# Moving the stages of the second half, the solver and the early weights to other slots of a hand-written timetable

## The chip, the cores and the metric

The kernel runs on one core of one Trainium2 chip. The metric is the device time of one execution in microseconds (us), from start to end of the program on that core. The core has five engines with a queue each, worked off in order: PE (matrix products), DVE, ACT and POOL (element-wise work), and SP, which here only issues DMA transfers. They meet through semaphores.

## The reference

Three parts follow each other. First a recurrence over 768 tokens for 4 x 8 heads of dimension 40, then two feed-forward layers over the 3072 tokens of width 320.

```python
for t in range(S):                       # S = 768, per batch and head, state 40x40
    y[t] = r[t] @ state
    Sa   = state @ a[t]
    state = state * w[t] - outer(Sa, b[t]) + outer(v[t], k[t])
x = y.transpose(0, 2, 1, 3).reshape(3072, 320)
h = relu(x @ moe_w_in);  x = (h * h) @ moe_w_out        # 320 -> 2048 -> 320
h = x @ moe2_w_in;       out = (h * cos(h)) @ moe2_w_out
```

## The kernel before

**Chunks.** The recurrence is cut into 12 chunks of 64 tokens (`C = 64`). Within a chunk the sequential part becomes the inverse of a triangular 64x64 matrix per head; only the 40x40 state goes from chunk to chunk. For chunk c+1, `gt` multiplies keys and decayed rows on PE and masks them on DVE into `ga`; `gt_out` writes the triangles to a scratch buffer `Ls` in HBM; `solve_load` reads them back as the tiles `L` and `T` (`lent` for chunk 1, which uses tiles lent by the weights), `corner_load` reads the off-diagonal corner `l21`. `solve` inverts the 32x32 diagonal blocks in 62 small multiply and add steps (L510, L513) and a copy (L517); for chunk 0 on DVE, for all others on POOL. `solve_store` writes the result out, `load_t` reads it back as `t11` and `tt`. `merge(h)` joins the diagonal blocks of one half of the heads: matmuls `pw`, an ACT copy to `l21`, matmuls `pt`, an ACT copy to `tt`.

**Stages.** The 16 head pairs go in four groups g, two to a half. `state(c, g)` is a generator with five stages: `pq` (state times r, not in chunk 0), `px`, `pu` (it uses `tt`, so it needs the merge), `py` with the new state `MT`, and `pm`, which transposes the state. `rv_load`, `mov_load` and `pmat` bring the inputs of a group, `y_store` stores the output of a half to `xs`.

**The timetable.** `period(c)` writes chunk c as 42 slots. `at(t, f)` puts a call into slot t; calls of one slot are emitted in the order in which they were registered. The order in which instructions are emitted is the order in each engine's queue; there is no other scheduler. In each slot, after the calls, `rate[t]` steps of the solver of chunk c+1 are emitted on POOL, then one step of the early weights (`w1`) or of the later ones (`w2`), and from chunk 2 on about 1.5 steps of the feed-forward layers (`mlp`, 64.2 of them to a period). What is left of the layers after chunk 11 runs alone until the end.

**Queues.** Nearly all transfers are issued by SP, one after the other. SP stands still at an instruction whose semaphore is not there yet, and all later transfers stand behind it. `solve_store` is such a place: it needs the end of the solver. The order of SP around it in chunks 2 and later is `y_store`, `solve_store`, `gt_out` (first half of chunk c+2), `load_t`, `gt_out`, then in the next period `load_kb` (`cin`, L379, 832 KB), `rv_load`, in even chunks four loads of `xf` for the layers (`load_x`), `gt_out` (second half), `rv_load`, `mov_load`, `solve_load`.

**Weights.** They arrive as 64-bit numbers. `Weights.first` turns the first 12 of 16 tiles of layer one into 32-bit ones while chunks 0 and 1 run: load, `clamp` on ACT (L171, L172), `bits` on DVE, `add` on POOL (L183), `split` on ACT (L210) and POOL (L215). Its jobs are 5 steps apart. `Vector` (the helper at L146 records all DVE work) inserts the DVE solver of chunk 0 between other DVE instructions.

Of the kernel before, what the change touches and what calls it, by code (L numbers as in the profile page):

```python
# [10 lines left out]
F32 = mybir.dt.float32  # L11
F32R = mybir.dt.float32r
# [146 lines left out]
class Weights:  # L159
# [58 lines left out]
    def first(self, last=NF, layer=0):  # L218

        m, nm = self.m, ("moe", "moe2")[layer]  # L220

        def job(f):
            st = {}

            def load():
                st["dst"] = m.weight_tile(layer, f)
                if self.raw:
                    st["w"] = m.p2.tile([128, 3, 512], F32R, tag=("xh", "xl")[f % 2], name="w1", bufs=1).bitcast(
                        I32).rearrange("p a b -> p (a b)")[:, 0:2 * NW].rearrange("p (a b) -> p a b", b=2)
                    self.load(nm, f, st["w"])  # L230

            def begin(c0, n):
                u = st[c0] = m.p2.tile([128, 512], F32, tag="g", name="u1", bufs=3)[:, 0:n]
                if self.raw:
                    self.clamp(st["w"][:, c0:c0 + n], u)
                else:
                    self.nc.sync.dma_start(u, self.i[nm][f, :, c0:c0 + n])

            out = [(0, load)]
            for t, c0, n in ((5, 0, 384), (6, 384, DM)):  # L240
                out.append((t, lambda c0=c0, n=n: begin(c0, n)))
                if self.raw:
                    out += [(t + 1, lambda c0=c0, n=n: self.bits(st["w"][:, c0:c0 + n], st[c0])),
                            (t + 2, lambda c0=c0, n=n: self.add(st["w"][:, c0:c0 + n], st[c0], st[c0]))]
                out.append((t + 4, lambda c0=c0: self.split(st["dst"], st[c0], c0, layer)))
            return out

        return self.stages([job(f) for f in range(last if self.raw else NF)], 5)

    def pieces(self, nm, tiles, period, end):  # L250

        if not self.raw:
            return iter(())

        def job(f, c0, n):
            st = {}

            def load():
                st["w"] = self.p.tile([128, 256, 2], I32, tag="w", name="w", bufs=2)[:, 0:n]
                self.load(nm, f, st["w"], c0)  # L260

            def clamp():
                st["u"] = self.p.tile([128, 256], F32, tag="u", name="u", bufs=2)[:, 0:n]
                self.clamp(st["w"], st["u"])

# [42 lines left out]
class Attn:  # L308
# [274 lines left out]
    def pmat(self, c, g):  # L583
# [18 lines left out]
        for r0, n, s0 in ((64, 40, 0), (0, 64, 4)):  # L602
            if c:
                nc.scalar.activation(mov[r0:r0 + n, s0:s0 + 4, 64:104], self.MT[g][r0:r0 + n], AF.Copy)
            else:
                nc.gpsimd.memset(mov[r0:r0 + n, s0:s0 + 4], 0.0)

    def y_store(self, c, half):
        for par, r0 in ((0, 64), (1, 0)):
# [3 lines left out]


    def state(self, c, g):
        nc = self.nc
        ga, rv, mov = self.ga[c, g // 2], self.rv.pop((c, g)), self.mov.pop((c, g))
        tt, kc, h4 = self.tt, self.kc, 4 * (g % 2)
# [39 lines left out]
        last = c == self.nch - 1  # L658
        if not last:
            self.vec.tensor_tensor(mt[0:104], yv[0:104, :, 64:104], mt[0:104], op=ALU.add)  # L660
        if c:
            self.vec.tensor_tensor(sz[0:104], yv[0:104, :, 0:64], sz[0:104], op=ALU.add)
        if not last:
            self.vec.tensor_tensor(mt[0:104], mt[0:104],
                                   self.lam[(c + 1) % 3][:, 4 * g:4 * g + 4, 64:65].to_broadcast([104, 4, 40]), op=ALU.mult)
        if g % 2 == 0:
            self.yt = self.p2.tile([128, 8, 64], F32, tag="yt", name="yt", bufs=1)
        yt = self.yt
# [275 lines left out]
def step(gen, n=1):  # L944
    for _ in range(n):
        if next(gen, 0) == 0:
            break

FIRST, RATE = 9, 64.2 / 42


class Program:
# [59 lines left out]
    def run(self):  # L1014
# [56 lines left out]
        self.vec.chain = A.solve(A.nc.vector)  # L1071
        for k in range(10):
            self.vec.credit = 6
            step(g1, 2 if k > 7 else 1)
            if k == 6:
                A.gt_out(1, 0, 0)
                A.gt_out(1, 0, 1)
            if k in (1, 3, 4, 5, 6, 7):
                step(self.w1)
            self.vec.finish()  # L1080
# [1 line left out]
        self.vec.finish()  # L1082
        A.solve_store()
        A.load_t()
        A.gt_out(1, 1, 0)
        A.gt_out(1, 1, 1)
        A.solve_load(1)
        step(self.dcs[2], 6)
        self.solver = A.solve(A.nc.gpsimd)
        for c in range(nch):  # L1090
# [13 lines left out]
    def period(self, c):  # L1104
# [7 lines left out]
            todo.setdefault(t, []).append((f, args))  # L1112

        for half in range(2):
            for k in range(5):
                for q in range(2):
                    at(20 * half + 4 * k, step, st[2 * half + q])
        for h, t0 in enumerate((5, 5) if c == 0 else (2, 2) if more else (4, 12)):
            mg = A.merge(h)
            at(t0, step, mg)  # L1120
            at(t0 + (4 if c and more else 2), step, mg)
        at(2, A.rv_load, c, 2)
        at(6, A.rv_load, c, 3)
        at(6, A.mov_load, c, 2)
        at(8, A.pmat, c, 2)
        at(14, A.mov_load, c, 3)
        at(16, A.pmat, c, 3)
        at(17, A.y_store, c, 0)
        at(37, A.y_store, c, 1)
        if more:  # L1130
            for t in (0, 1, 2):
                at(t, step, self.gts[c + 1])
# [6 lines left out]
            at(8 if c == 0 else 10, A.gt_in, c + 1, 1, 1)  # L1139
            if c:  # L1140
                at(6, A.solve_load, c + 1)
            at(8 if c == 0 else 6, A.corner_load, c + 1)
            first, last = (2, 26) if c == 0 else (9, 36)
            for t in range(first, last):
                rate[t] = 3 if t % 3 == 0 or c == 0 else 2
            rate[last] = 100
            at(28 if c == 0 else 37, A.solve_store)
            at(30 if c == 0 else 38, A.load_t)
            at(23, A.rv_load, c + 1, 0)
            at(25, A.rv_load, c + 1, 1)  # L1150
            at(26, A.mov_load, c + 1, 0)
# [3 lines left out]
        if c + 2 < nch:  # L1155
            for t in (0, 2, 3, 4, 5, 6, 7, 9):
                at(t, step, self.dcs[c + 2])
            if not A.ahead(c + 2):
                at(1, A.load_kb, c + 2)
                at(11, A.load_a, c + 2)  # L1160
            ck = A.compact_kb(c + 2)
            for t in (3, 5, 7, 10) if c == 0 else (10, 12, 14, 16):
                at(t, step, ck)
            at(20, A.compact_a, c + 2, 0)
            at(28, A.compact_a, c + 2, 1)
            self.gts.setdefault(c + 2, A.gt(c + 2))
            for t in (24, 25, 26, 32, 33, 34, 36, 37, 38):
                at(t, step, self.gts[c + 2])
            at(37, A.gt_out, c + 2, 0, 0)
            at(39, A.gt_out, c + 2, 0, 1)  # L1170
        if c + 3 < nch:
            self.dcs[c + 3] = A.decay(c + 3)
            at(18, A.load_w, c + 3)
            if A.ahead(c + 3):
                at(18, A.load_kb, c + 3)
                at(29, A.load_a, c + 3)
            for t in (34, 35, 36, 38, 40, 41):
                at(t, step, self.dcs[c + 3])
        for t in range(42):
            if more and t == 9 and c:  # L1180
# [107 lines left out]
```

## Time and profile before

| | us |
|---|---|
| median of 3 runs (lowest, highest) | 1274.33 (1273.46, 1278.36) |
| the profiled execution's own time | 1272.46 |
| its span, first to last instruction | 1270.7 |
| busy: PE, weight load of PE | 1065.8 (84%), 894.4 (70%) |
| busy: DVE, ACT, POOL | 696.7, 697.6, 690.3 (54 to 55% each) |
| mean granted clock of PE, share of full speed | 0.916 |

Shares are means over stages that have different limits: up to 199 us PE is busy for less than half of the time, after 845 us for nearly all of it. A line of a view names the source line, the engine, the operation and the tiles (out<-in); "idle before" is the time in which the engine had nothing to run, and the arrow names the event that ended it. A time of SP is the issue of a transfer, not the transfer.

### The profile page before, as it was taken

Reading aid. Unit: us, or ns where it says so; the run is one execution under the profiler, and the core shown is the slowest. Engines: PE = TensorE matmul, PEld = TensorE weight load, DVE = VectorE, ACT = ScalarE, POOL = GpSimd, SP = SyncE. Lnnn points to the kernel's source line nnn. Section 1 sums busy time; section 2 is a strip of 40 time slices with the busy share of each in tenths; the row PEclk is TensorE's granted clock in tenths of the full one; section 3 lists DMA queues with packets and bytes.
Section 4 is the critical chain, followed back from the end, with each engine's and each line's share of the span. In section 5 each row is a group of like instructions: output and inputs, shape, how many; then the busy total and the mean of one; then the engine's idle time right before and its main releaser. Section 6 shows DMA issues by size and latency. Waiting matters only on the chain.

```text
span 1270.7 us, 26720 instructions
## 1 busy us (share of the span) xinstructions
PE 1065.8 (84%) x10242; PEld 894.4 (70%) x10242; DVE 696.7 (55%) x1315; ACT 697.6 (55%) x1444; POOL 690.3 (54%) x1106
## 2 busy tenths in 40 slices
PE   3334636889889885989698989999999999999997
PEld 3334535667767764867577867777889999999996
DVE  7955964666657572666466634123696343443432
ACT  4223634566466554656456556547756555655553
POOL 3157693776638381838384838226796333333332
PEclk9996665888889897989799989999999999999999
DMA  8545726446372817463736362236101010101000
GB/s 197 126 100 144 178 82 123 104 97 150 60 172 64 166 44 160 101 140 73 167 92 145 69 133 74 59 99 210 68 19 46 1 47 1 47 9 38 1 21 24
DMA packets 267621, 115.96 MB, mean 91 GB/s; under 512 B 225036, under 2 KB 246028, under 8 KB 266652
## 3 DMA queue, kind: packets, MB, share of 16 engines
q1 hardware_dynamic: 265650, 113.47, 37.2%
q8 instruction: 83, 1.36, 0.4%
q10 hardware_dynamic: 1834, 0.69, 0.2%
q14 instruction: 54, 0.44, 0.1%
HBM read 88.42 MB, written 25.69 MB: 90 GB/s over the span
## 4 chain that ended last, share of the span: by engine, by line
PE 55%; POOL 18%; DVE 7%; DMA 7%; SPq 5%; issue 3%; ACT 3%; POOLq 0%; ACTq 0%; DVEq 0%
PE h L913 23%; PE pt L857 13%; PE po L867 9%; POOL T L513 5%; POOL ttmp L510 5%; DMA xf<-xs 3%; POOL gl L766 3%; POOL u L183 2%; PE pgt L459 2%; POOL ws L215 2%; DVE lam L146 2%; DVE u L146 1%; PE pu L644 1%; PE py L654 1%; DVE cin L146 1%
## 5 line engine op out<-in xcount | busy, mean ns | idle before, releaser
L913 PE MATMUL h<-xh,ws 128*128 128x512 f32 x960 | 328.8, 405 | 17.6 <-ACT g L763 17.0
L766 POOL TENSOR_TENSOR gl<-g,gh 128x512 fp32r<-128x512 f32 x96 | 126.0, 1313 | 201.5 <-ACT gh L765 150.4
L913 PE MATMUL h<-xl,ws 128*128 128x512 f32 x576 | 232.1, 403 | 0.2 <-DVE xl L146 0.2
L794 POOL TENSOR_TENSOR gl<-g,gh 128x512 fp32r<-128x512 f32 x96 | 125.1, 1303 | 190.9 <-ACT gh L793 161.5
L913 PEld LDWEIGHTS h<-xh,ws 128*128 128x128 f32 x960 | 182.4, 191 | 60.9 <-ACT g L763 21.6
L510 POOL TENSOR_TENSOR ttmp<-T,L 128x126 f32<-128x126 f32 (+22 forms) x310 | 123.6, 399 | 55.4 <-DMA L<-Ls 22.2
L867 PE MATMUL po<-gh,ws 128*128 128x512 f32 x480 | 142.9, 422 | 3.3 <-ACT o L813 2.7
L513 POOL TENSOR_TENSOR T<-T,ttmp 128x126 f32<-128x126 f32 (+22 forms) x310 | 132.1, 426 | 19.5
L857 PE MATMUL pt<-ws,gh 128*128 128x320 f32 x768 | 128.2, 309 | 0.5 <-DVE g L146 0.4
L763 ACT ACTIVATE g<-h 128x512 f32<-128x512 f32 x96 | 57.1, 594 | 129.5 <-PE h L913 106.8
L857 PEld LDWEIGHTS pt<-ws,gh 128*128 128x128 f32 x768 | 120.0, 188 | 8.3 <-DVE g L146 0.6
L913 PEld LDWEIGHTS h<-xl,ws 128*128 128x128 f32 x576 | 110.2, 191 | 20.7 <-DVE xl L146 1.4
L146 DVE SCALAR_TENSOR_TENSOR g<-n,h 128x512 f32<-128x512 int32 x96 | 65.9, 687 | 104.2 <-ACT n L774 101.7
L774 ACT ACTIVATE n<-h 128x512 int32<-128x512 f32 x96 | 57.3, 596 | 119.4 <-PE h L913 119.4
L146 DVE TENSOR_TENSOR mov<-pu,kc 64x416 f32<-64x416 f32 x96 | 56.5, 589 | 111.6 <-PE pu L645 99.1
L867 PEld LDWEIGHTS po<-gh,ws 128*128 128x128 f32 x480 | 93.4, 200 | 27.1 <-ACT o L813 3.3
L146 DVE TENSOR_TENSOR g<-g,h 128x512 f32<-128x512 f32 x96 | 65.8, 686 | 71.1 <-ACT g L778 71.0
L459 PE MATMUL pgt<-at,cin 40*128 40x104 f32 x768 | 71.0, 328 | 30.3 <-POOL at L439 12.8
L146 DVE TENSOR_SCALAR u<-u 128x160 f32<-128x160 f32 (+9 forms) x144 | 56.2, 391 | 64.0 <-ACT u L171 59.3
L459 PEld LDWEIGHTS pgt<-at,cin 40*128 40x128 f32 x768 | 61.5, 229 | 36.5 <-POOL at L439 13.5
L867 PE MATMUL po<-gl,ws 128*128 128x512 f32 x288 | 86.6, 405 | 0.0
L183 POOL TENSOR_TENSOR u<-u,w 128x384 int32<-128x384 int32 (+2 forms) x72 | 56.1, 779 | 53.7 <-DVE u L146 33.7
(112 smaller groups left out, 2310.3 us busy)
## 6 DMA issues: line engine op xcount, KB each, us to landing
w<-moe SPq DMA_DIRECT2D x20, 704.0 KB
rv<-rv SPq DMA_DIRECT2D x48, 256.0 KB
cin<-cin SPq DMA_DIRECT2D x8, 832.0 KB
Ls<-ga SPq DMA_DIRECT2D x48, 128.0 KB
L<-Ls SPq DMA_DIRECT2D x44, 128.0 KB
mov<-vt SPq DMA_DIRECT2D x96, 40.0 KB
xs<-yt SPq DMA_DIRECT2D x48, 80.0 KB
w<-moe SPq DMA_DIRECT2D x24, 160.0 KB
```

Source lines behind the costliest of these rows:

```text
L146: fn(*args, **kwargs)
L183: self.nc.gpsimd.tensor_tensor(t.bitcast(I32), u.bitcast(I32), w[:, :, 0], op=ALU.add)
L459: nc.tensor.matmul(pv[par][:, j], self.kb[r0:r0 + 40, p0 + j].rearrange("p h b -> p (h b)"), self.at[r0:r0 + 40, p0 + j], start=True, stop ...
L510: eng.tensor_tensor(tv, T[:, 0:r, j:j + 1].to_broadcast([128, r, n]), L[:, j:j + 1, j + 1:32].to_broadcast([128, r, n]), op=ALU.mult)
L513: eng.tensor_tensor(T[:, 0:r, j + 1:32], T[:, 0:r, j + 1:32], tv, op=ALU.add)
L763: nc.scalar.activation(g, h, AF.Relu)
L766: self.later.append((2, lambda: nc.gpsimd.tensor_tensor(gl, g, gh, op=ALU.subtract)))
L774: nc.scalar.activation(n, h, AF.Copy, bias=0.25, scale=float(np.float32(1.0 / (2.0 * np.pi))))
L794: nc.gpsimd.tensor_tensor(gl, g, gh, op=ALU.subtract)
L857: nc.tensor.matmul(self.pos[j][:, 0:DM], x[:, 128 * j:128 * j + 128], wo[:, DM * ws:DM * ws + DM], start=(f == 0 and x is gh and ws == 0), ...
L867: nc.tensor.matmul(self.pos[m], wo[:, 128 * ws:128 * ws + 128], x, start=(f == 0 and k in (0, 2, 4)), stop=(f == NF - 1 and k in (5, 6, 7)))
L913: nc.tensor.matmul(h, wi[:, ws], x[:, kt], start=(k == 0), stop=(k == 7))
```

## The change

The second half's stages go from slots 20, 24, 28, 32, 36 to 15, 19, 23, 27, 31 in chunks 0 and 1 (they stay in the others), the first half's from 0, 4, 8, 12, 16 to 0, 4, 10, 14, 18 in all chunks. The merge of half 0 stands at slots 5 and 8 and that of half 1 at 12 and 15, where both stood at 2 and 6 (5 and 7 in chunk 0; 4, 6 and 12, 14 in the last). The solver of chunks 2 and later begins at slot 8 for 9 and is all emitted by slot 33 for 36; `solve_store` and `load_t` go to slots 34 and 36 from 37 and 38. `load_kb` goes from slot 1 to 6, `corner_load` from 6 (8) to 17, `load_w` from 18 to 23, some others by a few slots. In the start-up, `gt` of chunk 1 takes two steps a turn where it took one, and its last `gt_out` and `solve_load(1)` stand inside the loop of the DVE solver, ahead of `solve_store`, where they stood behind `load_t`. The early weights get more steps between `clamp`, `bits`, `add` and `split` and a sixth temporary tile. The zero fill of `mov` of groups 2 and 3 in chunk 0 goes from POOL to DVE, and the state's scaling comes before the output's sum in `state`.

```diff
@@ first @@
+                if c0 == 0 and self.raw:
+                    u = st[c0] = m.p2.tile([128, 512], F32R, tag="gl", name="u0", bufs=3).bitcast(F32)[:, 0:n]
+                else:
+                    u = st[c0] = m.p2.tile([128, 512], F32, tag="g", name="u1", bufs=3)[:, 0:n]
-            out = [(0, load)]
+            out = [(2, load)]
-                    out += [(t + 1, lambda c0=c0, n=n: self.bits(...)),
-                            (t + 2, lambda c0=c0, n=n: self.add(...))]
-                out.append((t + 4, lambda c0=c0: self.split(st["dst"], st[c0], c0, layer)))
+                    out += [(t + 2, lambda c0=c0, n=n: self.bits(...)),
+                            (t + 3, lambda c0=c0, n=n: self.add(...))]
+                out.append((t + 8, lambda c0=c0: self.split(st["dst"], st[c0], c0, layer)))
@@ pieces @@
-            return [(0, load), (4, clamp), ...
+            return [(1, load), (4, clamp), ...
@@ pmat @@
-                nc.gpsimd.memset(mov[r0:r0 + n, s0:s0 + 4], 0.0)
+                (nc.gpsimd if g < 2 else self.vec).memset(mov[r0:r0 + n, s0:s0 + 4], 0.0)
@@ state @@
             self.vec.tensor_tensor(mt[0:104], yv[0:104, :, 64:104], mt[0:104], op=ALU.add)
+            self.vec.tensor_tensor(mt[0:104], mt[0:104], lam..., op=ALU.mult)
         if c:
             self.vec.tensor_tensor(sz[0:104], yv[0:104, :, 0:64], sz[0:104], op=ALU.add)
-        if not last:
-            self.vec.tensor_tensor(mt[0:104], mt[0:104], lam..., op=ALU.mult)
@@ run @@
-            step(g1, 2 if k > 7 else 1)
-            if k == 6:
+            step(g1, 2)
+            if k == 4:
                 A.gt_out(1, 0, 0)
                 A.gt_out(1, 0, 1)
+            if k == 7:
+                A.gt_out(1, 1, 0)
+                A.gt_out(1, 1, 1)
+                A.solve_load(1)
...
         A.solve_store()
         A.load_t()
-        A.gt_out(1, 1, 0)
-        A.gt_out(1, 1, 1)
-        A.solve_load(1)
@@ period @@
-            for k in range(5):
+            for t in ((15, 19, 23, 27, 31) if c < 2 else (20, 24, 28, 32, 36)) if half else (0, 4, 10, 14, 18):
                 for q in range(2):
-                    at(20 * half + 4 * k, step, st[2 * half + q])
+                    at(t, step, st[2 * half + q])
-        for h, t0 in enumerate((5, 5) if c == 0 else (2, 2) if more else (4, 12)):
+        for h, t0 in enumerate((5, 12)):
             mg = A.merge(h)
             at(t0, step, mg)
-            at(t0 + (4 if c and more else 2), step, mg)
+            at(t0 + 3, step, mg)
-        at(8, A.pmat, c, 2)
+        at(9, A.pmat, c, 2)
-        at(14, A.mov_load, c, 3)
-        at(16, A.pmat, c, 3)
-        at(17, A.y_store, c, 0)
-        at(37, A.y_store, c, 1)
+        at(14 if c < 2 else 16, A.mov_load, c, 3)
+        at(14 if c < 2 else 19, A.pmat, c, 3)
+        at(19, A.y_store, c, 0)
+        at(33 if c < 2 else 37, A.y_store, c, 1)
-            at(8 if c == 0 else 6, A.corner_load, c + 1)
-            first, last = (2, 26) if c == 0 else (9, 36)
+            at(17, A.corner_load, c + 1)
+            first, last = (2, 26) if c == 0 else (SOLVE, END)      # SOLVE, END = 8, 33
             for t in range(first, last):
-                rate[t] = 3 if t % 3 == 0 or c == 0 else 2
+                rate[t] = 2 if c and t % 3 == 0 else 3
             rate[last] = 100
-            at(28 if c == 0 else 37, A.solve_store)
-            at(30 if c == 0 else 38, A.load_t)
+            at(28 if c == 0 else END + 1, A.solve_store)
+            at(30 if c == 0 else END + 3, A.load_t)
-                at(1, A.load_kb, c + 2)
+                at(6, A.load_kb, c + 2)
-            for t in (3, 5, 7, 10) if c == 0 else (10, 12, 14, 16):
+            for t in (3, 5, 7, 10) if c == 0 else (16, 17, 19, 21):
                 at(t, step, ck)
-            at(20, A.compact_a, c + 2, 0)
+            at(22, A.compact_a, c + 2, 0)
-            at(18, A.load_w, c + 3)
+            at(23, A.load_w, c + 3)
```

## Rows read from the trace of the kernel before

**Rows 1.** Stretches: length, busy time of each engine, granted clock, DMA share, GB/s

```profile
199.30:276.70 77.40, 62.59 (x686) 49.54 (x682) 44.78 (x97) 42.80 (x104) 45.24 (x93) 0.76 0.50 110
276.70:793.20 516.50, 453.43 (x5581) 361.50 (x5580) 295.46 (x599) 302.12 (x690) 318.53 (x612) 0.92 0.52 114
845.00:1270.70 425.70, 413.94 (x2208) 367.47 (x2208) 203.18 (x287) 245.85 (x407) 196.78 (x170) 0.99 0.14 47
```

**Rows 2.** Waits of PE from 199 to 800 us: total, times, longest

```profile
PE pw L550 <- DMA t<-Tn: 38.6, 14, 9.2
...
PE pu L644 <- ACT tt L567: 16.6, 5, 7.4
```

**Rows 3.** The solver's last copy, by source line: ns, first and last start

```profile
L517 POOL COPY L<-T x10: 1032/1118/1378, 200.3 to 795.7; 64x512 f32<-64x512 f32 x10
```

**Rows 4.** Stretches: the solver of chunk 1, the gap behind it, that of chunk 2

```profile
77.20:116.10 38.90, 19.65 (x272) 17.20 (x272) 20.46 (x42) 10.36 (x25) 34.61 (x80) 0.74 0.38 103
116.10:146.20 30.10, 18.80 (x332) 17.07 (x334) 24.93 (x46) 23.39 (x60) 17.57 (x24) 0.60 0.84 190
146.20:201.40 55.20, 23.69 (x348) 21.21 (x345) 38.05 (x76) 24.39 (x64) 49.24 (x93) 0.64 0.27 81
```

**Rows 5.** Gaps from a solver's end to the next, chunks 2, 4, 6, 8: sum

```profile
sum 106.10, PE 71.36 PEld 59.54 DVE 43.24 ACT 51.35 POOL 12.00; mean PE 17.84 PEld 14.89 DVE 10.81 ACT 12.84 POOL 3.00
```

**Rows 6.** The same of chunks 3, 5, 7, 9

```profile
sum 94.20, PE 81.28 PEld 64.84 DVE 59.15 ACT 56.73 POOL 24.61; mean PE 20.32 PEld 16.21 DVE 14.79 ACT 14.18 POOL 6.15
```

**Rows 7.** All nine gaps: that of chunk 10, without `load_kb`, and the sum

```profile
735.90:757.70 21.80, 16.16 (x235) 12.74 (x234) 6.25 (x11) 10.81 (x24) 3.49 (x4) 0.77 0.88 184
sum 222.10, PE 168.79 PEld 137.12 DVE 108.64 ACT 118.89 POOL 40.10; mean PE 18.75 PEld 15.24 DVE 12.07 ACT 13.21 POOL 4.46
```

**Rows 8.** The nine stretches of the solver from 228.6 to 796.8 us, sum

```profile
sum 373.30, PE 348.73 PEld 275.02 DVE 230.06 ACT 227.09 POOL 325.38; mean PE 38.75 PEld 30.56 DVE 25.56 ACT 25.23 POOL 36.15
```

**Rows 9.** Transfers issued by SP from 410 to 436 us: start, us of issue

```profile
410.96 0.49 SPq L524 DMA_DIRECT2D Tn<-L  x1
...
419.01 0.35 SPq L379 DMA_DIRECT2D cin<-cin  x1
...
419.87 1.52 SPq L473 DMA_DIRECT2D Ls<-ga  x2
...
429.36 3.95 SPq L496 DMA_DIRECT2D L<-Ls  x4
```

**Rows 10.** The same from 735 to 757.8 us

```profile
744.39 2.60 SPq L716 DMA_DIRECT2D xf<-xs  x4
747.09 1.31 SPq L473 DMA_DIRECT2D Ls<-ga  x2
...
752.23 2.96 SPq L496 DMA_DIRECT2D L<-Ls  x4
```

**Rows 11.** Waits of SP from 199 to 800 us

```profile
SPq L524 <- POOL L L517: 51.4, 6, 13.2
...
SPq L581 <- PE py L656: 25.2, 8, 5.0
```

**Rows 12.** POOL by line, 435.7 to 476.2 us

```profile
L766 POOL TENSOR_TENSOR gl<-g,gh 128x512 fp32r<-128x512 f32 x6 | 7.7, 1276 | 0.0
```

**Rows 13.** Waits of POOL, 502.2 to 546.0 us

```profile
POOL gl L766 <- ACT gh L765: 3.4, 1, 3.4
```

**Rows 14.** POOL in order of time, 52 to 79 us

```profile
77.17 0.24 POOL L510 TENSOR_TENSOR lent<-lent 128x31 f32<-128x31 f32 x1 [22.01 <-DMA lent<-Ls]
```

**Rows 15.** SP in order of time, 44 to 75 us

```profile
66.68 2.26 SPq L473 DMA_DIRECT2D Ls<-ga  x2
```

**Rows 16.** DVE in order of time, 34 to 61 us

```profile
49.80 0.29 DVE L513 TENSOR_TENSOR T<-T,ttmp 128x126 f32<-128x126 f32 x1
```

**Rows 17.** SP's issues of `mov_load`, by source line: ns min/median/max

```profile
L581 SPq DMA_DIRECT2D mov<-vt x96: 533/602/2628, 33.7 to 814.2; - x96
```

**Rows 18.** The same of `y_store`

```profile
L610 SPq DMA_DIRECT2D xs<-yt x48: 287/398/519, 97.9 to 838.4; - x48
```

More of the change, by code (lines that the diff above doesn't have):

```diff
@@ L232, in begin @@
             def begin(c0, n):
-                u = st[c0] = m.p2.tile([128, 512], F32, tag="g", name="u1", bufs=3)[:, 0:n]
+                if c0 == 0 and self.raw:
+                    u = st[c0] = m.p2.tile([128, 512], F32R, tag="gl", name="u0", bufs=3).bitcast(F32)[:, 0:n]
+                else:
+                    u = st[c0] = m.p2.tile([128, 512], F32, tag="g", name="u1", bufs=3)[:, 0:n]
                 if self.raw:
@@ L242, in job @@
                 if self.raw:
-                    out += [(t + 1, lambda c0=c0, n=n: self.bits(st["w"][:, c0:c0 + n], st[c0])),
-                            (t + 2, lambda c0=c0, n=n: self.add(st["w"][:, c0:c0 + n], st[c0], st[c0]))]
-                out.append((t + 4, lambda c0=c0: self.split(st["dst"], st[c0], c0, layer)))
+                    out += [(t + 2, lambda c0=c0, n=n: self.bits(st["w"][:, c0:c0 + n], st[c0])),
+                            (t + 3, lambda c0=c0, n=n: self.add(st["w"][:, c0:c0 + n], st[c0], st[c0]))]
+                out.append((t + 8, lambda c0=c0: self.split(st["dst"], st[c0], c0, layer)))
             return out
@@ L264, in clamp @@
                 self.clamp(st["w"], st["u"])
-            return [(0, load), (4, clamp), (6, lambda: self.bits(st["w"], st["u"])),
+            return [(1, load), (4, clamp), (6, lambda: self.bits(st["w"], st["u"])),
                     (7, lambda: self.add(st["w"], st["u"], st["u"])), (period + 5, lambda: end(f, c0, st["u"]))]
@@ L660, in state @@
             self.vec.tensor_tensor(mt[0:104], yv[0:104, :, 64:104], mt[0:104], op=ALU.add)
+            self.vec.tensor_tensor(mt[0:104], mt[0:104],
+                                   self.lam[(c + 1) % 3][:, 4 * g:4 * g + 4, 64:65].to_broadcast([104, 4, 40]), op=ALU.mult)
         if c:
             self.vec.tensor_tensor(sz[0:104], yv[0:104, :, 0:64], sz[0:104], op=ALU.add)
-        if not last:
-            self.vec.tensor_tensor(mt[0:104], mt[0:104],
-                                   self.lam[(c + 1) % 3][:, 4 * g:4 * g + 4, 64:65].to_broadcast([104, 4, 40]), op=ALU.mult)
         if g % 2 == 0:
@@ L947, in step @@
             break
+SOLVE, END = 8, 33
 FIRST, RATE = 9, 64.2 / 42
@@ L1179, in period @@
         for t in range(42):
-            if more and t == 9 and c:
+            if more and t == SOLVE and c:
                 self.solver = A.solve(A.nc.gpsimd)
```

## Prediction, made before the change was run

> **What bounds the kernel now.** I read the stretches first [rows 1]. From 845 us on PE is busy for 413.9 of 425.7 us at a granted clock of 0.99, so nothing is to be had there, and no edit touches it. From 276.7 to 793.2 us, eight periods of 64.6 us each, PE is busy 453.4 us, or 56.7 a period: some 8 us of each period are idle. Since the layers' work is emitted at a fixed rate per slot, the work left after 845 us is fixed, and the time is the time at which the chunks end plus that remainder.
>
> Next the waits of PE say where the idle time lies [rows 2]: `pw`, the first matmuls of the merge, wait 38.6 us in 14 places for `t11`, and `pu` 16.6 us in 5 for the merged `tt`. Both are waits for the result of the solver. So I followed the solver. Its last copies start at 200.3 us and nine periods later at 795.7 us [rows 3]: 595.4 / 9 = 66.2 us a turn. A turn has two parts. The solver's own stretch is POOL work, 325.4 us busy of 373.3 us in nine stretches, 41.5 us each [rows 8]. Then POOL is nearly idle, 222.1 us in nine gaps, 24.7 us each [rows 7], until the next `L` is there. 41.5 + 24.7 = 66.2: solver and gap close a loop, and PE, with 56.7 us of work, is not in it.
>
> What fills a gap is SP. It stands at `solve_store` until POOL is done (51.4 us in 6 places, [rows 11]), and all that was emitted behind it then goes out one transfer at a time: from 410.96 us, at once behind the solver's end, to 421.4 us, when the second half's `Ls` has been issued. Only at 429.36 us is `Ls` landed so that `L` can be read [rows 9]; the four reads take 4.0 us to issue and some 2.4 more to land, and the next solver starts at 435.7 us. The gap is one queue's backlog and two round trips.
>
> Before 199 us another chain rules: the solver of chunk 1 starts at 77.17 us after POOL has stood 22.0 us for `L` [rows 14], because its `Ls` went out at 66.68 us, behind the stores and loads of chunk 0 [rows 15]. It ends at 116.1 us, the gap takes 30.1 us, and the solver of chunk 2 takes 55.2 us to 201.4 us with POOL busy 49.2 of them [rows 4].
>
> **The start-up.** With two steps of `gt` a turn all eight products of chunk 1's triangles are masked by the sixth turn. At 49.80 us DVE writes the 36th step of its solver, the last of that turn [rows 16]; four more masks, 0.58 us each, ahead of it put the last `ga` at about 52.4 us (an estimate). From the issue of `Ls` to the solver's start took 77.2 - 66.7 = 10.5 us [rows 14, 15], so the solver of chunk 1 would start at 62.9 us: **14.3 us** earlier. Its bounds are 0, if DVE is later than that, and 16.3, if the masks cost nothing. The solver's 38.9 us I leave: four zero fills leave POOL, a few steps of the early weights come in. The gap of 30.1 us [rows 4] should come nearer to 26.5, the mean of the even gaps [rows 5], since the second half of chunk 0 is five slots earlier and SP then waits less for DVE and PE: **4 us**, bounds 0 and 8.3 (the shortest gap, 21.8, [rows 7]). In the solver of chunk 2, 25 slots in place of 27 carry fewer steps of the weights: POOL is busy 49.2 us there and 36.2 in a mean later one [rows 4, 8], so 13 us are weights in excess, and 2/27 of it and of the layers' share is **1.7 us**. Looser lines for the early weights take ACT and DVE out of POOL's order; that is cover for these three terms, and I give it no time of its own, nor the order of the two DVE operations in `state`. Sum: 20 us, bounds 0 and 26.
>
> **The loop, nine turns.** In the gap the change takes `load_kb` from between the stores and `Ls`. One gap of before has no such load, that of chunk 10: 21.8 us [rows 7], against 106.1 / 4 = 26.5 for the other even ones [rows 5]; there `L` was issued 3.8 us after the last `Ls` (747.09 + 1.31 to 752.23, [rows 10]) and in the gap with the load 8.0 us after it [rows 9]. The odd gaps, 94.2 / 4 = 23.6 [rows 6], lack the four `xf` loads (2.6 us of issue, [rows 10]), so without `load_kb` they would be 19.2. But the change also puts four issues behind `solve_store` that stood ahead of it, two `mov_load` and two `y_store`: 2 x 0.60 + 2 x 0.40 = 2.0 us [rows 17, 18]. So even gaps go to 23.8 and odd to 21.2: 4 x 2.7 + 4 x 2.4 - 2.0 for that of chunk 10 = **18 us**. Bounds: if the load costs no more than its issue (0.35 us, [rows 9]), the gaps grow by 1.65 us each, -15 us; if the four issues stay hidden, +36.
>
> In the solver's stretch, 25 slots for 27 leave out 2/27 of `gl` (7.7 us in six, [rows 12]) and some of the weights, together about 0.7 us a turn: **6 us**. In even periods POOL also waits for `gh` while PE stands at `pu` (3.4 us in one of them, [rows 13]; at most 13.6 in four). With the merge two steps earlier against `pu` and split by halves I take a little over a third of it: **5 us**, bounds 0 and 13.6. That the solver ends at slot 33 gives nothing by itself: POOL is busy 325 of 373 us [rows 8], its end in time follows from its start. Nor do later merges shorten the loop: they let PE run some 3 slots further ahead before it waits. The last merge, at slot 5 for 4, gives **1 us** at the end.
>
> Where this cover goes: `corner_load`, `load_w`, `load_kb` and `compact_kb` move behind slots whose work they wait for anyway; if the kb read were late, `gt` from slot 24 on would be next, half a period later.
>
> **Sum.** 20 + 18 + 6 + 5 + 1 = 50 us. The profiled execution took 1272.5 us (its span 1270.7): 1222.5. The median of the runs is 1.9 us above it: **1224 us**.
>
> **A rule of the Trainium skill that is weighed here.** The rows show SP's issue as the stuff of the gap: from 410.96 to 421.4 us it issues without a pause [rows 9]. The page "DMA: Bandwidth & Descriptors", section "Issuing engines are not separate DMA queues", says that the time on a sequencer to initiate a DMA is usually small beside the DMA. By that rule the four issues moved behind `solve_store` would cost nothing, and the sum would be 1206 us.
>
> **The rivals.**
> 1. *PE becomes the bound.* If the loop gets shorter than PE's period, the periods stop at 56.7 us of work plus what remains idle, say 58.6 (an estimate from rows 1). Eight periods then gain 8 x (66.2 - 58.6) = 61 us, with 20 of the start-up and 1 at the end 82: 1192 us. For it: PE has 56.7 us [rows 1]. Against it: it needs another 4 us a turn out of gap or stretch that I can't name.
> 2. *Only the start-up gains.* The load's relief is eaten by the four issues, and POOL's denser order holds `gl` back: 1274.3 - 20 = 1254 us. For it: SP still stands at `solve_store` and POOL is as full as before.
> 3. *Slower.* `mov_load` now stands behind `solve_store`. It waited for PE's `py` 25.2 us in 8 places, 3.2 us each [rows 11], while SP had to wait for POOL anyway; behind it this wait would be in the loop. 3.2 + 2.0 us in nine turns without relief are 47 us, less 20 and 6: 1295 us. It decides from 2.9 us a turn on. Against it: in the gap PE already stands at the merge of the next period and waits for `t11` [rows 2], so that the `py` of slot 32 is done.
> 4. *Issues are free*, the four moved ones cost nothing: 9 x 2.0 = 18 us more, 1206 us. Against it: the rows of SP without a pause [rows 9].
> 5. *Nothing moves*, the start-up included: PE and ACT of chunk 0 then hold the solver's gap, 1274 us.
>
> **How the numbers follow.** Chances: the forecast (1210 to 1240) 0.49, rival 1 0.15, rival 2 0.20, rival 3 0.07, rival 4 0.06, rival 5 0.03. The range 1190 to 1256 leaves out rivals 3 and 5 and about half of rival 1. A half per cent (6.4 us) is what a measurement of this kernel can tell from no change. Faster: 0.49 + 0.15 + 0.20 + 0.06 = 0.90; the same 0.03; slower 0.07.
>
> **What the profile after would show.** POOL's first solver step near 63 us and its wait of 22 us gone; the copies (L517) at a spacing of about 63 us; `L` issued some 4 us after the last `Ls` and no `cin` between them; waits of `pw` nearly gone from PE, but idle time of PE still a few us a period, at `gl` or `g` if POOL's order holds it. The forecast is wrong if the spacing stays at 66 us (rival 2), if it falls under 60 (rival 1), or if SP waits for `py` at L581 behind L524 (rival 3).

## The result and the profile after

The changed kernel takes **1239.70 us** (median of 4 runs, 1237.93 to 1246.76) where the one before took 1274.57 in the same comparison: ratio 0.9732, 95% interval 0.9687 to 0.9776. The forecast was 1224 us in a range of 1190 to 1256. The gain was there, 35 us of the 50 foretold. The profiled execution took 1241.37 us, its span is 1239.5 us, 31.2 less than before. One run below, of e1_startup's six, fell in a slower state of the chip (1299.26 us at a granted clock of 0.807) and is left out of its median.

Of the changed kernel first the stretches (length, busy time of each engine, clock, DMA share, GB/s), to be held against [rows 1]. The windows are laid a little earlier, as the work is; the middle one holds the same eight periods, from the first `pq` of chunk 3 to that of chunk 11:

```profile
180.00:262.00 82.00, 60.67 (x667) 47.28 (x663) 47.04 (x95) 45.12 (x110) 54.89 (x109) 0.74 0.51 108
263.00:763.10 500.10, 462.82 (x5583) 359.06 (x5582) 300.91 (x603) 301.51 (x690) 319.49 (x616) 0.94 0.53 117
812.00:1220.00 408.00, 403.82 (x2153) 358.44 (x2152) 199.96 (x283) 240.96 (x399) 192.70 (x167) 1.00 0.14 47
```

PE does about the same work, 57.9 us a period for 56.7, in 62.5 us where it took 64.6; 4.7 us a period are still idle. The waits of PE from 180 to 800 us, against [rows 2]:

```profile
PE h L916 <- ACT g L766: 21.3, 10, 5.0
PE pt L566 <- ACT l L557: 10.3, 9, 3.7
```

`pw`, which led with 38.6 us, and `pu` are no longer among them: the merge no longer waits for the solver. The turn of the solver, its last copy by source line, against [rows 3]:

```profile
L520 POOL COPY L<-T x10: 1030/1100/1375, 187.0 to 761.4; 64x512 f32<-64x512 f32 x10
```

That is 574.4 / 9 = 63.8 us for 66.2. The nine stretches of the solver and the nine gaps, sums of two tables of windows, against [rows 8] and [rows 7]:

```profile
sum 353.40, PE 339.62 PEld 264.87 DVE 219.78 ACT 208.56 POOL 312.03; mean PE 37.74 PEld 29.43 DVE 24.42 ACT 23.17 POOL 34.67
...
sum 221.10, PE 182.08 PEld 140.16 DVE 123.03 ACT 135.15 POOL 54.96; mean PE 20.23 PEld 15.57 DVE 13.67 ACT 15.02 POOL 6.11
```

Here lies the surprise. The stretches gave 19.9 us, where 11 were foretold; the gaps gave 1.0, where 18 were. The start-up, against [rows 4]:

```profile
58.40:105.90 47.50, 27.85 (x476) 24.93 (x477) 40.45 (x85) 16.07 (x40) 38.13 (x75) 0.82 0.49 125
105.90:134.80 28.90, 13.88 (x193) 12.19 (x190) 22.63 (x37) 19.71 (x49) 18.32 (x26) 0.50 0.85 198
134.80:188.10 53.30, 30.80 (x418) 26.90 (x416) 44.44 (x77) 24.09 (x62) 49.16 (x91) 0.56 0.27 82
```

The solver of chunk 1 starts at 58.4 us, 18.8 earlier, after its `Ls` went out at 49.69 us for 66.68 in [rows 15]:

```profile
49.69 1.28 SPq L476 DMA_DIRECT2D Ls<-ga  x2
```

But it takes 47.5 us for 38.9; the solver of chunk 2 ends at 188.1 us, 13.3 earlier. So the account of the span is 13.3 + 19.9 + 1.0, less 3.0 that the part after the last solver grew: 31.2.

Why the gaps stayed is seen in the transfers that SP issues in one of them (start, us of issue):

```profile
386.93 0.48 SPq L527 DMA_DIRECT2D Tn<-L  x1
387.46 2.40 SPq L529 DMA_DIRECT2D Ts<-T  x2
390.02 1.25 SPq L584 DMA_DIRECT2D mov<-vt  x2
391.37 0.54 SPq L187 DMA_DIRECT2D w<-moe  x1
...
395.44 0.81 SPq L613 DMA_DIRECT2D xs<-yt  x2
396.35 1.33 SPq L476 DMA_DIRECT2D Ls<-ga  x2
...
399.42 1.26 SPq L476 DMA_DIRECT2D Ls<-ga  x2
...
402.77 0.60 SPq L496 DMA_DIRECT2D T<-kti  x1
403.48 4.08 SPq L499 DMA_DIRECT2D L<-Ls  x4
407.68 0.56 SPq L382 DMA_DIRECT2D cin<-cin  x1
```

`L` is read 2.8 us after the last `Ls` (399.42 + 1.26 to 403.48), where it was 8.0 us in [rows 9], and `cin` is out of the way. But `mov`, `xs` and one more `w` now stand behind `solve_store`: 29 issues without a pause from 386.93 to 407.56 us. From the solver's end to the end of the last `Ls` issue it is 13.8 us for 10.5 in the gap of [rows 9], and from the read of `L` to the solver's first step 7.4 for 6.3: 13.8 + 2.8 + 7.4 = 24.0 us for 10.5 + 8.0 + 6.3 = 24.8.

### The profile page after: what moved, and what is told of

It reads as the page before. It is cut to its first block, busy times and chain, and to the rows that moved or that the text cites. A ratio compares the mean times of both kernels' runs of the same rounds, so it can differ in the third digit from the quotient of the medians.

```text
span 1239.5 us, 26732 instructions
## 1 busy us (share of the span) xinstructions
PE 1079.6 (87%) x10242; PEld 894.5 (72%) x10242; DVE 712.9 (58%) x1319; ACT 695.9 (56%) x1444; POOL 695.1 (56%) x1102
## 5 line engine op out<-in xcount | busy, mean ns | idle before, releaser
L916 PE MATMUL h<-xh,ws 128*128 128x512 f32 x960 | 332.9, 409 | 26.0 <-ACT g L766 21.3
L769 POOL TENSOR_TENSOR gl<-g,gh 128x512 fp32r<-128x512 f32 x96 | 127.1, 1324 | 174.2 <-ACT gh L768 132.2
L516 POOL TENSOR_TENSOR T<-T,ttmp 128x126 f32<-128x126 f32 (+22 forms) x310 | 130.0, 419 | 20.1
L766 ACT ACTIVATE g<-h 128x512 f32<-128x512 f32 x96 | 57.2, 596 | 123.5 <-PE h L916 114.9
L777 ACT ACTIVATE n<-h 128x512 int32<-128x512 f32 x96 | 57.2, 596 | 119.5 <-PE h L916 119.5
L462 PE MATMUL pgt<-at,cin 40*128 40x104 f32 x768 | 74.2, 335 | 39.3 <-DVE at L146 13.0
L870 PEld LDWEIGHTS po<-gh,ws 128*128 128x128 f32 x480 | 89.7, 193 | 24.6 <-ACT o L816 3.1
L462 PEld LDWEIGHTS pgt<-at,cin 40*128 40x128 f32 x768 | 64.4, 235 | 45.7 <-issue 14.4
L870 PE MATMUL po<-gl,ws 128*128 128x512 f32 x288 | 90.2, 410 | 0.0
L183 POOL TENSOR_TENSOR u<-u,w 128x384 int32<-128x384 int32 (+2 forms) x72 | 57.5, 799 | 56.1 <-DMA Ls<-ga 23.4
L781 ACT ACTIVATE g<-g,kc 128x512 f32<-128x512 f32 x96 | 69.7, 726 | 26.5 <-DVE g L146 25.6
```

The costliest lines, as they stand in the source:

```text
L183: self.nc.gpsimd.tensor_tensor(t.bitcast(I32), u.bitcast(I32), w[:, :, 0], op=ALU.add)
L462: nc.tensor.matmul(pv[par][:, j], self.kb[r0:r0 + 40, p0 + j].rearrange("p h b -> p (h b)"), self.at[r0:r0 + 40, p0 + j], start=True, stop ...
L516: eng.tensor_tensor(T[:, 0:r, j + 1:32], T[:, 0:r, j + 1:32], tv, op=ALU.add)
L766: nc.scalar.activation(g, h, AF.Relu)
L769: self.later.append((2, lambda: nc.gpsimd.tensor_tensor(gl, g, gh, op=ALU.subtract)))
L781: nc.scalar.activation(g, g, AF.Sin, bias=self.kc[:, K_QT:K_QT + 1])
```

## The experiments

A gap and a stretch are counted as in [rows 7, 8], up to the end of the closing copy. In some expectations below they are counted from the last step's end instead, without that copy: there the changed kernel has stretches of 342.6 and gaps of 231.8 us. All ratios are to the kernel before, run beside each.

| run | median us | ratio (95%) | turn | stretches | gaps |
|---|---|---|---|---|---|
| before | 1274.57 | | 66.2 | 373.3 | 222.1 |
| after | 1239.70 | 0.973 (0.969 to 0.978) | 63.8 | 353.4 | 221.1 |
| e1_startup | 1265.83 | 0.993 (0.990 to 0.996) | 66.9 | 381.3 | 220.4 |
| e2_later | 1247.71 | 0.979 (0.976 to 0.983) | 63.1 | 353.5 | 214.4 |
| e3_kb1 | 1262.71 | 0.991 (0.988 to 0.994) | 66.3 | 351.2 | 245.6 |
| e4_store37 | 1228.22 | 0.964 (0.960 to 0.967) | 62.1 | 356.2 | 202.9 |
| e5_store40 | 1225.08 | 0.960 (0.957 to 0.964) | 62.7 | 357.6 | 206.6 |
| e6_bits | 1243.68 | 0.976 (0.972 to 0.981) | 63.6 | 352.3 | 220.4 |
| e7_rate | 1236.16 | 0.969 (0.966 to 0.973) | 64.1 | 379.7 | 196.8 |
| e8_merge | 1229.20 | 0.964 (0.961 to 0.968) | 62.7 | 356.4 | 207.9 |
| e9_xf | 1244.67 | 0.977 (0.975 to 0.980) | 64.2 | 367.1 | 210.3 |
| e10_xf_bits | 1241.28 | 0.975 (0.972 to 0.978) | 63.9 | 365.5 | 209.7 |
| e11_xf_t40 | 1242.16 | 0.975 (0.973 to 0.978) | 63.7 | 364.8 | 208.5 |
| e12_no_xf | 1218.77 | 0.955 (0.953 to 0.958) | 61.2 | 358.0 | 192.8 |

Turn, stretches and gaps are of one profiled execution each. For eight of the kernels the nine gaps are cut further, by SP's and POOL's order of time, in us: how late after the solver's end SP issues `solve_store` (`Tn<-L`), from there to the end of the last issue of `Ls` ahead of `L`, from there to the read of `L`, and from that read to the solver's first step.

| sum of nine gaps | before | after | e3 | e4 | e5 | e7 | e9 | e12 |
|---|---|---|---|---|---|---|---|---|
| `solve_store` late | 1.9 | 1.1 | 1.2 | 6.0 | 17.4 | 0.2 | 4.8 | 5.9 |
| to the last `Ls` issued | 125.3 | 134.5 | 151.2 | 111.9 | 100.2 | 110.0 | 99.9 | 108.0 |
| to the read of `L` | 43.5 | 28.3 | 40.6 | 29.9 | 30.1 | 29.8 | 20.7 | 24.4 |
| to the first step | 51.4 | 57.2 | 52.5 | 55.0 | 58.9 | 56.9 | 84.9 | 54.6 |

**e1_startup, e2_later: the two halves of the change.** The change is cut at chunk 2: e1 has the start-up, the weights' lines and `period_a` of after and `period_b` of before, e2 the other way round. The order of the two DVE operations in `state` goes with the start-up and holds for all chunks: e1 has the changed one throughout, e2 the old one.

```diff
+    def period(self, c):
+        (self.period_a if c < 2 else self.period_b)(c)
```

> The changed start-up, weights' lines and chunks 0 and 1, with the timetable of before from chunk 2 on. Loop theory (solver stretch and gap close a loop; what the start-up wins is carried to the end): the solver of chunk 2 ends some 13 us earlier, as in the changed kernel (188.1 for 201.4 us), the later turns stay at 66.2 us, the time falls by about 13 us (1261). As the prediction sized it, the start-up is worth 20 us (1254). Rival (PE's order sets the later periods and the start-up's gain is lost in them): within 3 us of the kernel before (1272 to 1277). Rival (all of the gain comes from the start-up): about 1241.

> The start-up and chunks 0 and 1 of before, with the changed timetable from chunk 2 on. Loop theory: turns of about 63.8 us for 66.2 in eight or nine turns, the time falls by 15 to 20 us (1255 to 1260), and this and the run with the changed start-up alone add up to the whole of 35 us. Rival (the later timetable gives nothing without the earlier start): 1272 to 1277. As the prediction sized the loop it would be 30 us (1244).

Measured: -9.1 and -27.2 us (against 1274.89 in their comparison), together 36.3 for the whole change's 34.9. The halves add up; neither needs the other. In e1 the solver of chunk 2 ends at 188.4 us, 13 earlier as in the changed kernel, but the later stretches grew by 8 us and took part of that back. The start-up is worth about half of the 20 us of the prediction; the loop, above the 15 to 20 us expected here, nearly the 30 it got, though by other terms.

**e3_kb1: the price of `load_kb` in the gap.**

```diff
-                at(6, A.load_kb, c + 2)
+                at(1 if c >= 2 else 6, A.load_kb, c + 2)
```

> The changed kernel with load_kb back at slot 1 from chunk 2 on, so that it stands again between the stores and the last Ls. If the prediction's price for it holds (2.7 and 4.4 us a gap), the gaps are 27 to 31 us in eight turns, the time rises by 20 to 28 us to 1260 to 1268. Rival A (only its issue counts, since in the gap SP issues without a pause from 386.9 to 407.6 us and the landing is covered by other issues): 0.35 to 0.7 us a turn, 3 to 6 us, 1243 to 1246. Rival B (the gap does not set the time): within 3 us of 1240.

Measured: 23.0 us slower than after, within the 20 to 28 expected, and rival A falls. The gaps are 24.5 us longer; eight of them have the load, 3.1 us each, two thirds of the 4.4 to 4.7 that the prediction took off for the load (the 2.7 above has the moved issues in it already). SP in one such gap of e3_kb1 (start, us of issue):

```profile
407.48 0.36 SPq L382 DMA_DIRECT2D cin<-cin  x1
...
408.82 1.35 SPq L476 DMA_DIRECT2D Ls<-ga  x2
...
414.20 0.33 SPq L496 DMA_DIRECT2D T<-kti  x1
416.43 3.08 SPq L499 DMA_DIRECT2D L<-Ls  x4
```

The load's issue is 0.36 us; its price is in what stands behind it. In this gap the read of `L` starts 6.3 us after the last `Ls` (408.82 + 1.35 to 416.43), 2.8 us without the load: of the pauses, SP stands 2.0 us at the load of `T` until `cin` has landed and 1.8 at that of `L` until `Ls` has. In the four gaps where the loads of `xf` follow `cin`, the read of `L` comes hardly later, but the issue of the last `Ls` itself takes 3.7 to 4.7 us. The same gap of e3_kb1 and of after:

```profile
606.55 3.94 SPq L476 DMA_DIRECT2D Ls<-ga  x2
...
587.94 1.31 SPq L476 DMA_DIRECT2D Ls<-ga  x2
```

Over the nine gaps e3_kb1 has 16.7 us more up to the last `Ls`, 12.3 more from there to the read of `L`, and 4.7 less behind it.

**e4_store37: the moved issues.** `solve_store` and `load_t` go back behind `mov_load` and `y_store`; the rest of the change stays.

```diff
-            at(28 if c == 0 else END + 1, A.solve_store)
-            at(30 if c == 0 else END + 3, A.load_t)
+            at(28 if c == 0 else END + 1 if c == 1 else 37, A.solve_store)
+            at(30 if c == 0 else END + 3 if c == 1 else 38, A.load_t)
```

> The changed kernel with solve_store at slot 37 and load_t at 38 from chunk 2 on, as before, so that mov_load, y_store and the weights' loads of slots 34 to 37 are issued ahead of the store again; nothing else is moved back. Loop theory with SP's issues as the gap: each gap falls by the four moved issues, 2.0 us, and by one or two loads of weights, 0.5 to 1 us, nine turns: 18 to 27 us, 1213 to 1222. Rival A (PE's work per period is the bound by now): within 3 us of 1240. Rival B (mov_load or y_store then hold SP for PE longer than POOL takes): slower, 1245 or more.

Measured: the gaps fall by 18.2 us in nine, 2.0 us each (weights' transfers of slots 34 to 37 are in it too). The time is 1228.22, 11.5 us better than the change as made and short of the 18 expected, in part by the 2.8 us that the stretches grew. That the 2.0 is the number of the prediction is partly chance: the part behind `solve_store` fell by 23.1 us (220.0 to 196.9), and 4.9 of it were lost, since SP now reaches `solve_store` itself 6.0 us late, for 1.1. Rival 4 of the prediction falls here: the issues are not free. The Trainium skill, "DMA: Bandwidth & Descriptors", "Issuing engines are not separate DMA queues", says that the time to initiate a DMA is usually small beside the DMA. That may hold for each of the 29 issues counted above, 0.7 us in the mean, and yet they add up, since they stand in a row behind one wait; the 1206 us drawn from it did not come.

**e5_store40: more of them ahead of the store.** The same edit with 40 and 41.

> The changed kernel with solve_store at slot 40 and load_t at 41 from chunk 2 on, so that the triangles' stores of slots 37 and 39 and the weights' transfers of slots 37 to 40 stand ahead of it too. With the store at 37 the nine gaps fell from 231.8 to 213.4 us and SP issued without a pause in them. Theory (the gap is the sum of the issues behind solve_store): two to four issues of 0.6 us less than with the store at 37, gaps of 195 to 205 us, turns of about 61 us, 1214 to 1222. Rival A (T now comes later to the merges, PE stands at pw, and the turn is set over T, merge, gt): pw waits 3 us or more a turn and the time is 1226 to 1240. Rival B (PE's 57 us of work plus its waits for g are the bound): the gap falls but the stretch grows by as much, 1225 to 1231.

Measured: 1225.08, not to be told from e4_store37; the gaps did not fall further. Waits of SP from 180 to 800 us in e5_store40:

```profile
SPq L286 <- POOL T L516: 67.5, 7, 14.1
...
SPq L527 <- POOL L L520: 28.7, 5, 17.8
```

These are two rows of several: a row is of one releaser. With all rows of POOL summed, SP stands at `solve_store` (L527) for POOL 110.6 us in the changed kernel, 44.4 in e4_store37 and 34.9 here, and at the store of converted weights (`w2f`, L286), which waits for POOL's `add` among the solver's steps (L516), 82.8, 103.4 and 124.9. In the kernel before, the longest of SP's waits for POOL was neither of them but that of the weights' loads (L187), 146.5 us in 29 places. The theory was right in its part: from `solve_store` to the last `Ls` issued it is 11.7 us less than in e4_store37. But SP comes 11.4 us later to `solve_store` (17.4 for 6.0): the gates of SP are several, and what is put ahead of one meets the next. Rival A did not come (`pw` does not wait 3 us a turn), and of rival B only the time did (1225.08, at the edge of its range): the gaps did not fall.

**e6_bits: solver 1's wait.**

```diff
+        step(self.w1)
         step(self.dcs[2], 6)
...
-            elif c or t % 2 == 0:
+            elif c or t and t % 2 == 0:
```

> The changed kernel with the early weights' step of slot 0 taken ahead of the six scans of chunk 2's decay. Theory (solver 1 is 8.6 us longer than before because POOL stands 4.8 us at the add for DVE's bits behind the scans, and the rest because its operations take longer beside a busy DVE): the wait falls to 2 us or less, solver 1's stretch from 46.4 to about 43.5 us, and the later turns start 3 us earlier: 1236 to 1238. Rival (chunk 0's PE and ACT set the start of chunk 2's solver): within 1.5 us of 1240.

What it removes is in POOL's order of time in the changed kernel:

```profile
59.13 0.23 POOL L513 TENSOR_TENSOR lent<-lent 128x30 f32<-128x30 f32 x1
64.16 1.50 POOL L183 TENSOR_TENSOR u<-u,w 128x384 int32<-128x384 int32 x1 [4.79 <-DVE lam L146]
```

Measured: the wait fell from 4.8 to 1.3 us, the stretch from 47.5 to 45.2 (58.4 to 103.6 us), and the solver of chunk 2 ended 2.2 us earlier in the profile. The time, 1243.68 with runs from 1234.71 to 1247.52, can't tell a gain of that size: inconclusive.

**e7_rate, e8_merge: where the stretches' gain comes from.** Both stand on e4_store37. In e7 the solver has its old slots from chunk 2 on, in e8 the merges have theirs (the first two lines below are of e7, the last two of e8).

```diff
+            first, last = (2, 26) if c == 0 else (SOLVE, END) if c == 1 else (9, 36)
+                rate[t] = (3 if t % 3 == 0 else 2) if c > 1 else 2 if c and t % 3 == 0 else 3
...
+        for h, t0 in enumerate((2, 2) if c > 1 and more else (4, 12) if c > 1 else (5, 12)):
+            at(t0 + (4 if c > 1 and more else 2 if c > 1 else 3), step, mg)
```

> The changed kernel with solve_store at 37 and load_t at 38 (1228.2 us) and, from chunk 2 on, the solver's slots as before: from 9, three steps in each third slot and two in the others, to 36. If the fewer slots are what shortened the stretch: the prediction gave them 0.7 us a turn, so nine stretches of about 352 us for 345.7 and 1234; if they are the whole of it, about 365 us and 1247. Rival (the slots give nothing, the merges and what POOL no longer waits for do): 345 to 347 us and within 3 us of 1228.

> The changed kernel with solve_store at 37 and load_t at 38 (1228.2 us) and, from chunk 2 on, the merges as before: both halves at slot 2 and their second steps at 6. Theory of the prediction (POOL waited for gh in even periods while PE stood at pu, and the later and split merges give some 5 us of that back): the stretches rise by about 5 us, pu waits come back to 3 us an even period, 1233. Rival A (the merges are the whole of the stretches' 20 us): 1245 or more. Rival B (nothing hangs on the merges now that the gap is shorter, or they even help since T is needed earlier): within 3 us of 1228.

Measured: with the old slots the stretches are 379.7 us, 23.5 more; with the old merges 356.4, 0.2 more, and a time 1.0 us away. The slots are the whole of it, and the rival of e8's expectation that nothing hangs on the merges came true, in a kernel with the store at 37. In e7_rate the stretches rose as if the slots were the whole, the time (1236.16) as the lower of the two estimates had it. First the two sums of e7_rate (all, then `gl` of POOL, L769, alone):

```profile
sum 379.70, PE 365.25 PEld 285.97 DVE 242.18 ACT 234.86 POOL 329.44; mean PE 40.58 PEld 31.77 DVE 26.91 ACT 26.10 POOL 36.60
...
sum 379.70, POOL 66.33; mean POOL 7.37
```

and the same of e4_store37:

```profile
sum 356.20, PE 339.12 PEld 264.30 DVE 224.71 ACT 211.24 POOL 313.51; mean PE 37.68 PEld 29.37 DVE 24.97 ACT 23.47 POOL 34.83
...
sum 356.20, POOL 56.27; mean POOL 6.25
```

Of 23.5 us, 10.1 are `gl` operations that are no longer among the solver's steps, 5.9 (329.4 to 313.5 less these) POOL's other work, mostly the solver's own steps, and 7.6 are time in which POOL was not busy (50.3 to 42.7). The gaps pay 6.1 us of it back (196.8 to 202.9), and 5.8 of that is SP coming late to `solve_store` (6.0 for 0.2): the shorter stretch ends in two gaps before SP has got there. By medians the slots are worth 7.9 us; the two profiled executions differ by 13.4, e7's being the slowest of its four runs and e4's next to its fastest.

**e9_xf, e10_xf_bits, e11_xf_t40, e12_no_xf: less ahead of the last `Ls`.** On e4_store37, from chunk 2 on:

```diff
-        at(2, A.rv_load, c, 2)
+        at(4 if c > 1 else 2, A.rv_load, c, 2)
...
-                at(6, A.solve_load, c + 1)
+                at(4 if c > 1 else 6, A.solve_load, c + 1)
...
-            if c % 2 == 0 and c and t == 2:
+            if c % 2 == 0 and c and t == (4 if c > 2 else 2):
```

The last two lines move `load_x` and are not in e12. e10 adds the edit of e6, e11 has `load_t` at 40.

> The changed kernel with solve_store at 37 and load_t at 38 (1228.2 us) and, from chunk 2 on, less ahead of the last Ls in the gap: load_x two slots later (slot 4, chunk 4 on), rv_load of the third group at slot 4, and solve_load at 4 ahead of rv_load and mov_load of slot 6. Theory (the gap is the sum of SP's issues): 2.6 us of xf issues and 0.6 of rv less before the last Ls in four even gaps, 0.6 in the others, and the order of L behind a landing of about 3 us gives nothing more: gaps of about 198 us for 213.4, 1213 to 1217. Rival A (PE bound: 57 us of work a turn and its waits for g): the gap falls, the stretch or pw's waits grow by as much, the turn stays at 61.5 to 62.1 us and the time within 3 us of 1228. Rival B (the layer then waits for its x): slower than 1231.

> The kernel before in this list with the early weights' step of slot 0 taken ahead of the six scans of chunk 2's decay, as in the run that took it alone (there solver 1's stretch fell from 46.4 to 44.1 us in the profile, but the time could not be told from 1240). If the loop carries a gain of the start-up through: 2 us below the kernel before in this list; rival: no difference.

> The first kernel of this list with load_t at slot 40 in place of 38, the store still at 37. Theory (SP's stand at load_t for the landing of Ts, 1 us, and two Ls issues come out of the chain to L, T comes some 2 us later to the merge): gaps 1 us a turn shorter, 5 to 9 us below the first kernel. Rival (the turn is set through T, merge and PE by now): pw's waits grow and the time is the same or up to 5 us longer.

> The kernel with load_x at slot 4, rv_load and solve_load at 4 (1244.7 us) with load_x back at slot 2. In that one's trace ACT stands 7.8 us for xf ahead of xh from 462 us on, and PE 54.7 us in 11 places for g in all chunks. Theory (the later load_x is the whole of its loss; ahead of L only 0.6 us of rv_load is gone, and the landing of Ls takes the place of rv_load and mov_load): 1223 to 1229, waits of h for g back at some 25 to 30 us, gaps 205 to 214 us. Rival (solve_load ahead of rv_load and mov_load of slot 6 is at fault, since the state stages then wait for mov): 1236 or more, with waits of pp or pm for rv or mov.

Measured: e9_xf is 16 us slower than its base, against the theory, and as rival B had it. ACT of e9_xf in order of time, and then its PE's waits from 180 to 800 us:

```profile
462.77 0.80 ACT L557 ACTIVATE l<-pw 32x256 f32<-32x256 f32 x2
471.32 0.63 ACT L733 ACTIVATE xh<-xf 128x512 fp32r<-128x512 f32 x1 [7.75 <-DMA xf<-xs]
```

```profile
PE h L916 <- ACT g L766: 54.7, 11, 11.0
```

ACT stands 7.8 us for `xf`, and `g`, behind it in ACT's queue, holds PE. The way into the loop is over POOL, whose queue has a `gl` ahead of the solver's first step; POOL of e9_xf:

```profile
476.69 1.27 POOL L769 TENSOR_TENSOR gl<-g,gh 128x512 fp32r<-128x512 f32 x1 [18.34 <-ACT gh L768]
477.92 0.24 POOL L513 TENSOR_TENSOR ttmp<-T,L 128x31 f32<-128x31 f32 x1
```

So in four gaps the first step comes 13 to 15 us after the read of `L`, for some 6 in the others. Up to that read the gaps did fall, as the theory had it (22.4 us less in nine than in e4_store37); behind it they grew by 29.9. With `load_x` back in its place and the other two edits kept, e12_no_xf, PE's wait is as before:

```profile
PE h L916 <- ACT g L766: 26.6, 13, 4.2
```

and the time is 1218.77, 9.5 below e4_store37, with gaps 10.1 us shorter. That is more than the 0.6 us a turn of one `rv_load`, which the 3.9 us up to the last `Ls` are near to: the landing of `Ls` was put at 3 us there, and in one gap of this run `L` starts 2.15 us after the last `Ls` has been issued (514.35 + 1.27 to 517.77). So the reads of `rv` and `mov` that stood between had lengthened the gap, by 5.5 us in nine. The differences of e10 and e11 to e9, 3.4 and 2.5 us, are within what the intervals leave open. e12_no_xf is the fastest version here.

## Why the prediction was right, and where it was off

- **The loop** (stretch plus gap sets the turn, PE is not in it): right. The two halves of the change add up, gaps lengthened (e3) and shortened (e4) came out in the time, and PE lost `pw`. Rival 1 did not come: even at 61.2 us a turn (e12) the 58.6 of a PE-bound period is not reached. Rival 2 fell with e2, rivals 3 and 5 with the result; SP's wait for `py` at L584 was 10.1 us in 3 places, not one in each gap.
- **Loop gaps, 18 us: the term that was mis-sized.** It was 36 of relief less 18 for the moved issues; 1.0 was measured. The relief measured 24.5 (e3): 3.1 us a gap for the 4.5 read from the comparison of gaps with the load to the one without it and to the distance of `Ls` and `L`. That distance is 8.0 us in the gap of [rows 9], but this is the longest of the eight with the load; their mean is 5.0, against 3.8 in the one without. The issues measured 18.2 (e4), or 23.1 if SP's late coming to `solve_store`, which before and after hardly have (1.9 and 1.1), is not counted against them. 24.5 - 23.1 leaves 1.4; these are differences of single profiled executions.
- **Stretches, 6 + 5 us:** the change gained 19.9 there, and the slots were worth 23.5 (e7 against e4), not 6; the prediction took 2/27 of `gl` and some weights, when 10.1 us of `gl` left and 7.6 us of POOL's idle time with it. POOL's wait for `gh` at `gl` inside the nine stretches did fall, from 10.7 us to 3.0, but by the slots and not by the merges, to which the 5 us were given: it is 8.5 with the old slots (e7) and 1.5 with the old merges (e8). That later merges don't shorten the loop was right.
- **Start-up, 20 us:** the solver's start came 18.8 us earlier, above the bound of 16.3 (16.6 by its own rows). The last `Ls` went out at 49.69 us, where their data were put at 52.4, and from there to the first step it took 8.8 us for 10.5. The gap gave 1.2 for 4, the second stretch 1.9 for 1.7. The step that failed is "the solver's 38.9 us I leave": it grew by 8.6 us, 4.8 of it the wait that e6 shows; the early weights' lines that were given no time of their own cost here. Of the 13.3 us by 188 us, e1 shows 9.1 in the time.
- **The end, 1 us:** the part after the last solver grew by 3.0 instead.

So by the profiled spans the sum was over by 6.7 us in the start-up, 17 in the gaps and 4.0 at the end, and under by 8.9 in the stretches; the time was 15.7 us above the forecast. It was in part luck that the time came out inside the forecast's 1210 to 1240, by 0.3 us: a stretch term off by nearly two made up for half of what the gaps fell short. Of the signs named, the missing wait of `pw`, the spacing of 63.8 us and no `cin` ahead of `L` came.

What stays open: why e1's later stretches grew by 8 us though their timetable is that of before (e1 has the changed order of the two DVE operations in `state` there, which no run varied alone), and what solver 1's remaining 3.8 us are due to; its steps alone took 2.7 us longer, see the last section.

## What to carry to other kernels

Where one queue stands at a wait and issues its backlog afterwards, count each issue behind the wait, and ask of a large transfer not what its issue takes but what is issued and lands behind it. Cut a part of a loop further before you price it: two of its pieces can move against each other, and their sum then agrees by chance. A second gate on the same queue takes over when work is moved ahead of the first; sum a wait over all its rows before saying which gate it is. A load moved later is safe only where its reader's queue holds nothing urgent.

## What the runs showed of the hardware

- A transfer's issue says little of its price: 0.36 us of issue for `cin` cost 3.1 us a gap, through what stood behind it: in one gap 6.3 us from the last `Ls` to the read of `L` for 2.8, in another 3.94 us of issue for the last `Ls` for 1.31 (e3_kb1 against after).
- The solver's 62 steps on POOL, the same instructions on the same shapes, were slower in the first stretch of after, where DVE is busy for 40.5 of 47.5 us, than of before, where it is for 20.5 of 38.9: 26.7 us for 24.0. By line, four groups of after, and then the three of before that are made up alike (the shapes of L183 differ):

```profile
L516 POOL TENSOR_TENSOR lent<-lent 128x126 f32<-128x126 f32 (+22 forms) x31 | 13.7, 442 | 2.1
L513 POOL TENSOR_TENSOR lent<-lent 128x126 f32<-128x126 f32 (+22 forms) x31 | 13.0, 418 | 12.1 <-DMA lent<-Ls 9.8
L215 POOL TENSOR_TENSOR ws<-u,ws 128x256 fp32r<-128x256 f32 (+2 forms) x8 | 5.9, 758 | 0.0
L183 POOL TENSOR_TENSOR u<-u,w 128x384 int32<-128x384 int32 (+1 forms) x4 | 5.0, 1240 | 4.8 <-DVE lam L146 4.8
```

```profile
L513 POOL TENSOR_TENSOR lent<-lent 128x126 f32<-128x126 f32 (+22 forms) x31 | 12.7, 411 | 1.8
L510 POOL TENSOR_TENSOR lent<-lent 128x126 f32<-128x126 f32 (+22 forms) x31 | 11.3, 366 | 24.2 <-DMA lent<-Ls 22.0
L215 POOL TENSOR_TENSOR ws<-u,ws 128x256 fp32r<-128x256 f32 (+2 forms) x8 | 4.3, 555 | 0.0
```

The Trainium skill, "GPSIMD Engine Reference", "1. Specifications", says that POOL's interfaces to SBUF are shared with VectorE, with contention from DVE instructions in a 2-port mode or with two inputs from SBUF. The rows agree with contention, but which of DVE's instructions were of these kinds was not looked at, no run here varied DVE's work alone, and the transfers were busier too (DMA share 0.49 for 0.38): the cause is argued and not shown.

- The granted clock from 262 to 759 us was 0.94 in after, and 0.97 in e4_store37 and e12_no_xf, where PE is idle for less; whether the busier PE is the reason was not tried. The four runs of the changed kernel differ with it: 1241.37 and 1246.76 us at a mean of 0.920 and 0.918, 1238.04 and 1237.93 at 0.929 and 0.932. Differences of a few us between two kernels are no larger than that.
